# A spectral mixer and a mixture of experts on one core: where indirect DMAs, small transform pieces and logits stand in the order

## The chip, the cores and the metric

The kernel runs on one core of one Trainium2 chip, in one launch. The metric is the time of an execution on the device in microseconds (us); less is better. The time before is the median of three runs, 1420.36 us.

## The reference

```python
X = np.fft.rfft(x, axis=1)                       # x: 8 batches, 2496 tokens, 256 channels
y = np.fft.irfft(X * (filt_r + 1j * filt_i)[None], n=2496, axis=1)
x = y.reshape(8 * 2496, 256)                     # N = 19968 rows
logits = x @ w_gate                              # 8 experts
expert_idx = np.argmax(logits, axis=1)
gate_w = softmax(logits)[np.arange(N), expert_idx]
# each row goes through the one expert that it chose:
h = np.maximum(x_e @ w1[e], 0.0)                 # 256 -> 1024
y_e = h @ w2[e]                                  # 1024 -> 256
out = gate_w[:, None] * y                        # rows back in their own order
```

All of it is in float32.

## The kernel before

Each batch goes through a transform in four stages on TensorE, with the filter on VectorE and GpSimd in the middle: stage a (`bank<-fin,ta`), stage b (`bank<-fin,tb`), stage c (`bank<-zz,tc`) and stage d (`bank<-fin,td`). Batches 2 to 7 use half-size forms of these stages, whose matmuls fill a part of the array each, so that several run side by side: 64x64 tiles for a and d ("quarter" in the code), 64x32 and 32x64 tiles for b and c ("eighth"). A batch has 22 tiles of tokens, in six chunks of up to four. After stage d, each chunk of these batches is transposed on VectorE (`turn_y`, `yt`), multiplied by the gate's weights in 128x32 tiles (`block_logits`, `bank<-yt,wb`, "row" in the code), copied out of PSUM (`ls`) and turned back by a small matmul (`block_back`, `bank<-sel,ls`). Every two chunks, `route` finds the experts, gates and places of 8 tiles of tokens, and each tile's rows are scattered to a table in DRAM sorted by expert (`rows<-yo,row`): a small copy puts the gate into the row (`yo<-gts`, on ScalarE or GpSimd), and GpSimd issues an indirect DMA. When a batch is scattered, `tile_map` makes the list of expert tiles that are now full, in a chain of operations on 1x8 to 1x40 elements on VectorE (`av_i`, `av`, `end`, `add`, `past`, `erow`, `rrow`).

Expert tiles of up to 512 rows follow: SyncE loads rows (`xg`) and weights (`w1t`, `w2t`), VectorE turns the rows (`xT`), GpSimd makes sums of weights (`wsum`), TensorE makes the products (`bank<-xT,w1t`, `bank<-sums,wsum`, `bank<-xT,wsum`, `bank<-w2t,hT`), and result rows (`ys`) go to the output by an indirect DMA from GpSimd (`out_dram<-ys,ng`). These products are TensorE's filler: while batch k is transformed, tiles of batches before it are multiplied. Behind the last batch's scatters only expert tiles are left.

All engines take their instructions in the order in which this program writes them. A planner (class `Order`) sets the order while it is written: it keeps an estimated time for each engine and each tile, and the main loop takes the step that is due and ready by these estimates. `DUE` is a table of some 60 numbers: due times of the steps and thresholds. Four parts of the planner matter here. `count` estimates what an instruction takes. `flush` issues stores, and result DMAs once their rows are ready by the estimate (or four are waiting). `side` advances `route`, and halts it at a scatter while GpSimd's estimated time is over `DUE["side"]` ahead of TensorE's. The main loop picks the next step; if the last one was of a small shape, a step of the same shape goes first (`same`). The page gives line 484 for every instruction (484 is the helper through which the planner issues), so tiles' names are used instead.

Of the kernel before, what the change touches and what calls it, by code (L numbers as in the profile page):

```python
# [20 lines left out]
P = 128  # L21
# [194 lines left out]
def most_pieces(groups):  # L216
# [11 lines left out]
    "rush": -48.714,  # L228
    "alike": 0.017917,
    "mix": 25.552,  # L230
    "x_engine": 0.28811,
    "h_engine": 0.86204,
    "w2_engine": 0.11423,
    "f_engine": 0.085965,
    "gate_engine": 1.019,
    "flush": 0.57109,
    "send": 0.29959,
    "side": 2.3746,
    "idle": 2.8515,
    "share_most": 5.3092,  # L240
    "share_least": 1.471,
    "share_kept": 315.71,
    "tile": 35.828,
    "planes_by": 0.76561,
    "planes": -0.87134,
    "signs_by": 0.33611,
    "signs": -0.1406,
    "late_b": 0.31336,
    "late_s": 0.55053,
    "late_c": 0.040383,  # L250
    "filter": 0.021597,
    "filter_by": 0.0482,
    "third": 0.29655,
    "filter_ahead": 0.73168,
    "early_b": -0.23633,
    "early_by": 1.3308,
    "early_c": 0.020642,
    "first_0": -0.32219,
    "first": -0.06639,
    "first_by": 0.85692,  # L260
    "fold": 0.1218,
    "fold_ahead": 0.16979,
    "fourth_0_by": 0.87411,
    "fourth_0": 0.23401,
    "fourth_1": 0.42245,
    "fourth": 0.32009,
    "fourth_by": 0.78703,
    "turn": -0.083147,
    "logits": 0.013028,
    "back": 0.010872,  # L270
    "later_0": 0.22158,
    "later": 0.066514,
    "lists_0": 1.5128,
    "lists": 1.1508,
    "x_ahead": 0.71159,
    "stored": 0.7191,
    "w1_sums": 0.67379,
    "h_sums": 2.3401,
    "w2_sums": 1.2229,
    "w2_pace": 2.1142,  # L280
    "begin": 1.4709,
    "same": 0.30193,
# [3 lines left out]
class Order:  # L286
# [9 lines left out]
    PORT = 0.13  # L296

    def __init__(self, nc):
# [6 lines left out]
        self.kind = ""  # L305
        self.done, self.used, self.slots, self.ahead = {}, {}, {}, {}
# [77 lines left out]
    def count(self, engine, op, args, named):  # L384
# [25 lines left out]
        if op.endswith("dma_start"):  # L410
# [6 lines left out]
            self.t[engine] = start + self.ISSUE[engine]  # L417
            took = self.transfer(out, named["in_"]) * (1.1544 if engine == "gpsimd" else 1.0)
# [7 lines left out]
        elif engine == "tensor":  # L426
# [105 lines left out]
def kernel(  # L532
# [584 lines left out]
    def block_logits(b, c):  # L1117

        n = CH[c][1]
        yt = yts.pop((b, c))  # L1120
        lt = bank()[:, :n * CT]
        for r in range(2):
            for q in range(4):
                j = 4 * r + q
                mm(lt[q * CT:(q + 1) * CT], lhsT=wb[:, j, :], rhs=yt[:, :, j * CT:(j + 1) * CT], start=(r == 0), stop=(r == 1))
        ls = outs["s", b, c] = sb.tile([P, 4 * CT], F32, tag="ls", name="ls", bufs=1)[:, :n * CT]
        evac(ls, lt, n * CT)

    def block_back(b, c):

        n = CH[c][1] * CT
        p = bank()[:n, :CT]
        mm(p, lhsT=outs.pop(("s", b, c)), rhs=sel, start=True, stop=True)
        evac(lgs[b][:n, 4 * c:4 * c + 4].rearrange("p i e -> p (i e)"), p, CT)
# [28 lines left out]
    def route(b, c0, c1):  # L1163
# [670 lines left out]
    def slot(k):  # L1834
# [48 lines left out]
        if k + 1 < B:  # L1883
            for c in range(nch):
                at = (DUE["first_0"] if k == 0 else DUE["first"]) + DUE["first_by"] * c / nch
                late_x = k + 1 >= BA
                if late_x:
                    steps.append((max(at - DUE["fold"], 0.001), lambda c=c: fold_x(k + 1, c), ("x", k + 1, c), 0.0, "x", lambda c=c: t["vector"] < t["tensor"] + DUE["fold_ahead"] and [ins["x", k + 1, c]]))
                steps.append((max(at, 0.002), lambda c=c: stage_a(k + 1, c), None if late_x else ("x", k + 1, c), (0.29 if late_x else 0.43) * CH[c][1], "a",
                              lambda c=c: (not late_x or (k + 1, c) in folded) and [tables["ta"], ins["x", k + 1, c], sb.free("st") - 0.9]))  # L1890
                if late_x:
                    KINDS[steps[-1][1]] = "quarter"
        if k > 0:
            for c in range(nch + 3):
# [10 lines left out]
                if by_blocks(k - 1):  # L1905
                    if 1 <= c <= nch:
                        steps.append((at + DUE["turn"], lambda c=c: turn_y(k - 1, c - 1), None, 0.0, "d", lambda c=c: len(yts) < 2 and ("odd", k - 1, c - 1) not in outs and [outs["o", k - 1, c - 1]]))
                        steps.append((at + DUE["logits"], lambda c=c: block_logits(k - 1, c - 1), None, 0.5, "l", lambda c=c: [yts[k - 1, c - 1]]))
                        KINDS[steps[-1][1]] = "row"
                        steps.append((at + DUE["logits"] + DUE["back"], lambda c=c: block_back(k - 1, c - 1), None, 0.15, "l", lambda c=c: [outs["s", k - 1, c - 1]]))  # L1910
                        if c % 2 == 0:
                            steps.append((at + DUE["logits"] + DUE["back"] + 0.0005, lambda c=c: sides.append(route(k - 1, c - 2, c)), None, 0.0, "l"))
# [63 lines left out]

    def side():

        while sides and not (held[0] == "pool" and t["gpsimd"] > t["tensor"] + DUE["side"]):
# [211 lines left out]
    with tc.manual_schedule(engines=None):  # L2191
# [38 lines left out]
        while fs or any(heads):  # L2230
# [79 lines left out]
```

## Time and profile before

| | |
|---|---|
| median of three runs | 1420.36 us (1420.33 to 1420.42) |
| the profiled execution | 1419.16 us |
| its span, first instruction to last | 1417.3 us |
| TensorE busy with matmuls | 1355.6 us (96%) |
| VectorE, GpSimd, ScalarE busy | 905.5, 801.3, 579.8 us |
| indirect DMAs on GpSimd, rows scattered and results | 176 and 153 |

The page lists the busy time of each engine and the costliest groups of instructions. A matmul's end is modelled and overlaps the next one's start, so the time that a group takes of TensorE is read as the distance from its start to the start of what follows. The chain that ended last says nothing here: it holds only the last output DMA. What can be read are TensorE's own waits, stretches where its groups take longer than the same groups elsewhere, and its granted clock.

### The profile page before, as it was taken

Reading aid. Unit: us, or ns where it says so; the run is one execution under the profiler, and the core shown is the slowest. Engines: PE = TensorE matmul, PEld = TensorE weight load, DVE = VectorE, ACT = ScalarE, POOL = GpSimd, SP = SyncE. Lnnn points to the kernel's source line nnn. Section 1 sums busy time; section 2 is a strip of 40 time slices with the busy share of each in tenths; the row PEclk is TensorE's granted clock in tenths of the full one; section 3 lists DMA queues with packets and bytes.
Section 4 is the critical chain, followed back from the end, with each engine's and each line's share of the span. In section 5 each row is a group of like instructions: output and inputs, shape, how many; then the busy total and the mean of one; then the engine's idle time right before and its main releaser. Section 6 shows DMA issues by size and latency. Waiting matters only on the chain. (4 is left out here: it accounts for less than half of the span.)

```text
span 1417.3 us, 28606 instructions
## 1 busy us (share of the span) xinstructions
PE 1355.6 (96%) x9706; PEld 1052.9 (74%) x9706; DVE 905.5 (64%) x1717; ACT 579.8 (41%) x1451; POOL 801.3 (57%) x1084
## 2 busy tenths in 40 slices
PE   8998879999999989999999999998999999999997
PEld 6664546767766767767876787787888888999997
DVE  4756778657877866877767656354554455545674
ACT  3556325434444434435434344343333333344433
POOL 3436664756565368547756663665555554444465
PEclk9999999999999999999999999999999999999999
DMA  8967769569866965685574654566777646654342
GB/s 322 301 184 258 249 219 264 180 184 277 240 209 191 273 194 185 184 259 165 184 225 148 179 172 140 150 180 240 232 224 223 218 147 194 189 190 117 105 151 69
DMA packets 209717, 283.96 MB, mean 200 GB/s; under 512 B 116692, under 2 KB 154431, under 8 KB 209566
## 3 DMA queue, kind: packets, MB, share of 16 engines
q1 hardware_dynamic: 192510, 237.41, 55.4%
q0 software_dynamic: 17056, 44.67, 8.7%
q8 instruction: 79, 1.29, 0.4%
q14 instruction: 72, 0.59, 0.1%
HBM read 202.67 MB, written 79.60 MB: 199 GB/s over the span
## 5 line engine op out<-in xcount | busy, mean ns | idle before, releaser
L484 PE MATMUL bank<-w2t,hT 128*128 128x256 f32 (+1 forms) x2592 | 471.2, 336 | 1.0 <-DVE w2t L484 0.5
L484 PEld LDWEIGHTS bank<-w2t,hT 128*128 128x128 f32 x2592 | 407.7, 191 | 54.7 <-issue 8.0
L484 DVE TENSOR_TENSOR hT<-bank,hT 128x512 f32<-128x512 f32 (+1 forms) x228 | 147.2, 659 | 217.3 <-PE bank L484 184.7
L484 POOL DMA_INDIRECT out_dram<-ys,ng x153 | 163.9, 1071 | 136.5 <-ACT ys L484 57.3
L484 POOL DMA_INDIRECT rows<-yo,row x176 | 182.9, 1039 | 83.1 <-ACT yo L484 29.9
L484 ACT ACTIVATE ys<-bank,ng 128x128 f32<-128x128 f32 (+1 forms) x206 | 80.5, 414 | 354.0 <-PE bank L484 309.1
L484 POOL TENSOR_TENSOR wsum<-w1t 128x256 f32<-128x256 f32 x152 | 126.6, 833 | 170.0 <-PE bank L484 155.0
L484 ACT COPY hT<-bank 128x512 f32<-128x512 f32 (+1 forms) x228 | 127.9, 565 | 122.0 <-PE bank L484 100.7
L484 PE MATMUL bank<-sums,wsum 128*128 128x256 f32 (+1 forms) x608 | 158.5, 383 | 11.5 <-ACT hT L484 5.6
L484 PE MATMUL bank<-xT,w1t 128*128 128x256 f32 (+1 forms) x672 | 157.0, 378 | 1.7 <-issue 1.4
L484 PE MATMUL bank<-xT,wsum 128*128 128x256 f32 (+1 forms) x608 | 154.0, 376 | 1.4 <-DVE hT L484 1.3
L484 PEld LDWEIGHTS bank<-xT,w1t 128*128 128x128 f32 x672 | 121.5, 193 | 27.6 <-issue 7.4
L484 ACT ACTIVATE hT<-hT 128x512 f32<-128x512 f32 (+2 forms) x152 | 123.6, 813 | 42.6 <-DVE hT L484 41.0
L484 PEld LDWEIGHTS bank<-sums,wsum 128*128 128x128 f32 x608 | 103.9, 191 | 46.4 <-issue 24.2
L484 PEld LDWEIGHTS bank<-xT,wsum 128*128 128x128 f32 x608 | 109.1, 192 | 24.2 <-issue 8.2
L484 ACT ACTIVATE hT<-bank 128x512 f32<-128x512 f32 (+2 forms) x141 | 64.3, 468 | 43.8 <-PE bank L484 40.8
L484 PE MATMUL bank<-sums,w1t 128*128 128x256 f32 (+1 forms) x304 | 75.8, 372 | 0.6 <-ACT hT L484 0.6
L484 POOL TENSOR_TENSOR wsum<-wsum,w1t 128x256 f32<-128x256 f32 x76 | 65.0, 855 | 6.0
L484 POOL TENSOR_TENSOR wsum<-w1t,wsum 128x256 f32<-128x256 f32 x76 | 63.2, 832 | 0.0
L484 PEld LDWEIGHTS bank<-sums,w1t 128*128 128x128 f32 x304 | 54.7, 192 | 10.3 <-ACT hT L484 1.4
L484 DVE SCALAR_TENSOR_TENSOR ys<-bank,ng,ys 128x128 f32<-128x128 f32 x84 | 26.2, 346 | 54.8 <-PE bank L484 35.6
L484 DVE TENSOR_TENSOR sums<-xT,sums 128x256 f32<-128x256 f32 (+1 forms) x76 | 59.6, 785 | 1.9
(191 smaller groups left out, 1914.2 us busy)
## 6 DMA issues: line engine op xcount, KB each, us to landing
w1t<-in_moe_w_dram SPq DMA_DIRECT2D x80, 512.0 KB
w2t<-in_moe_w_dram SPq DMA_DIRECT2D x80, 512.0 KB
fin<-in_x_dram SPq DMA_DIRECT2D x39, 512.0 KB
fin<-zd SPq DMA_DIRECT2D x35, 512.0 KB
xg<-rows SPq DMA_DIRECT2D x136, 128.0 KB
ud<-uo SPq DMA_DIRECT2D x30, 512.0 KB
zd<-zo SPq DMA_DIRECT2D x31, 480.0 KB
fin<-ud SPq DMA_DIRECT2D x24, 512.0 KB
```

What stands on the lines that cost most here:

```text
L484: return real(*args, **named)
```

## The change

1. The planner notes indirect DMAs on GpSimd: one that starts less than 1.6 us after the one before continues a run (`trains`). Small-shape matmuls near a run are estimated longer, by a table (`TRAIN`).
2. In the main loop, steps of the "eighth" and "row" shapes are put last in the choice while a run of two or more stands near TensorE's time, and the preference for the same shape is off then.
3. A scatter of `route`, and a result DMA while transform steps are left, also waits, in the planner's time, until a gap after the indirect DMA before has passed (`paced`): 1.3223 us for batches 0 and 1, 2.4431 us for the others. No semaphore or delay is added on the chip: only the place in the order changes. `hold` exists too, but with its threshold of 99 it never holds.
4. `block_logits` and `block_back` take two chunks at a time: 18 visits in place of 36 each, with the same matmuls; one copy out of PSUM in place of two for the logits.
5. Stage a of a folded pair of chunks waits for both folds. The cost of a change of shape depends on the shape (`SWITCH`), and all numbers of `DUE` are new.

The matmuls and the bytes moved are the same; 25 of the gate copies go from ScalarE to GpSimd, and a few additions change places between VectorE and GpSimd.

```diff
 DUE = {
+    "train": 1.5001,
+    "hold": 99,
+    "pace": 2.4431,
+    "pace_0": 1.3223,
...
-    "logits": 0.013028,
+    "logits": 0.046351,
...
+    TRAIN = {"": (1.0, 1.0, 1.0, 1.12, 1.12, 2.55), "row": (1.36, 1.16, 1.66, 1.66, 1.66, 1.66),
+             "quarter": (1.0, 1.0, 1.0, 1.0, 1.0, 1.0), "eighth": (1.0, 2.6, 3.25, 3.25, 3.25, 3.25)}
+    gap = 0.0
+    SWITCH = {"": 0.09, "row": 0.15, "quarter": 0.3, "eighth": 0.41}
...
+            if engine == "gpsimd":
+                at, n = self.trains[-1]
+                self.trains = self.trains[-9:] + [(start, n + 1 if start - at < 1.6 else 1)]
+                self.paced = start + self.gap
...
-                took += 0.12
+                took += self.SWITCH[self.kind]
...
+            at, n = next((r for r in reversed(self.trains) if r[0] <= start), (-9.0, 0))
+            if n and start - at < 1.35:
+                took *= self.TRAIN[kind][min(n, 6) - 1]
...
-        while sends and (nc.ready(sends[0][0]) <= t["tensor"] + DUE["send"] or len(sends) > 3):
+        while sends and (max(nc.ready(sends[0][0]), nc.paced if fs else 0.0) <= t["tensor"] + DUE["send"] and not hold() or len(sends) > 3):
             send()
...
     def block_logits(b, c):
...
+        for i in range(c, c + 2):
+            n = CH[i][1]
+            yt = yts.pop((b, i))
+            for r in range(2):
+                for q in range(4):
+                    j = 4 * r + q
+                    mm(lt[q * CT:(q + 1) * CT, at:at + n * CT], lhsT=wb[:, j, :], rhs=yt[:, :, j * CT:(j + 1) * CT], start=(r == 0), stop=(r == 1))
+            at += n * CT
...
+        nc.gap = DUE["pace_0"] if b < 2 else DUE["pace"]
+        yield "pool"
...
-        while sides and not (held[0] == "pool" and t["gpsimd"] > t["tensor"] + DUE["side"]):
+        while sides and not (held[0] == "pool" and (max(t["gpsimd"], nc.paced) > t["tensor"] + DUE["side"] or hold())):
...
+            trains = sum(t["tensor"] - 1.35 < at < t["tensor"] + 0.5 and n > DUE["train"] for at, n in nc.trains)
+            if trains:
+                choice.sort(key=lambda c: not isinstance(c[0], int) and KINDS.get(c[0][1]) in ("eighth", "row"))
...
-            if same:
+            if same and not (trains and nc.kind in ("eighth", "row")):
```

Three places show how the order moves. In the rows, `xN` counts equal instructions that follow each other.

TensorE, in the part of the program where batch 2's first stage-d pieces stand (`fin,td`), before:

```order
L484 MATMUL bank<-xT,w1t 128x256 x10
L484 MATMUL bank<-w2t,hT 128x256 x16
L484 MATMUL bank<-fin,td 64x512 x4
L484 MATMUL bank<-fin,ta 64x512 x8
L484 MATMUL bank<-fin,td 64x512 x4
L484 MATMUL bank<-yt,wb 32x128 x8
L484 MATMUL bank<-xT,w1t 128x256 x4
L484 MATMUL bank<-fin,ta 64x512 x4
L484 MATMUL bank<-fin,td 64x512 x4
```

And the same part now:

```order
L500 MATMUL bank<-fin,ta 64x512 x8
L500 MATMUL bank<-w2t,hT 128x256 x8
L500 MATMUL bank<-fin,td 64x512 x4
L500 MATMUL bank<-xT,w1t 128x256 x4
L500 MATMUL bank<-fin,td 64x512 x4
L500 MATMUL bank<-sums,wsum 128x256 x2
L500 MATMUL bank<-xT,wsum 128x256 x2
L500 MATMUL bank<-sums,wsum 128x256 x2
L500 MATMUL bank<-sums,w1t 128x256 x2
L500 MATMUL bank<-xT,w1t 128x256 x4
L500 MATMUL bank<-fin,td 64x512 x4
```

The first logits (`yt,wb`), which stood right behind the second stage-d piece, are no longer in this stretch: they come with nine rows between them and the second stage-d piece, as 16 matmuls of two chunks together; expert products stand between the stage-d pieces.

GpSimd, in the same part of the program, from the last scatter of batch 1 on (`zp`, `zz`: the filter's products; `xT`, `wsum`: sums for expert tiles), before:

```order
L484 DMA rows<-yo,row 163840x264
L484 TENSOR_TENSOR zp<-zz,hl 128x1024
L484 TENSOR_TENSOR zz<-zz,hl 128x1024
L484 TENSOR_TENSOR zp<-zp,zz 128x512 x2
L484 DMA out_dram<-ys,ng 19968x256
L484 MEMSET lg 64x32
L484 DMA out_dram<-ys,ng 19968x256
L484 TENSOR_TENSOR zp<-zz,hl 128x1024
L484 TENSOR_TENSOR zz<-zz,hl 128x1024
L484 TENSOR_TENSOR xT<-xT 128x256
```

And now:

```order
L500 DMA rows<-yo,row 163840x264
L500 MEMSET tau_77 1x1
L500 DMA out_dram<-ys,ng 19968x256
L500 MEMSET tau_77 1x1
L500 DMA out_dram<-ys,ng 19968x256
L500 TENSOR_TENSOR xT<-xT 128x256
L500 TENSOR_TENSOR wsum<-w1t 128x256
L500 TENSOR_TENSOR wsum<-wsum,w1t 128x256
```

Between the last scatter and the sum for the next expert tile (`xT`) no filter product stands on GpSimd any more, where six operations on 512 or 1024 columns stood.

GpSimd, where the last six tiles of batch 4 are scattered, before:

```order
L484 DMA out_dram<-ys,ng 19968x256
L484 TENSOR_SCALAR yo<-lids 128x4x4
L484 TENSOR_SCALAR yo<-lids 128x2x4
L484 DMA rows<-yo,row 163840x264
L484 MEMSET tau_77 1x1
L484 DMA rows<-yo,row 163840x264
L484 MEMSET tau_77 1x1
L484 DMA rows<-yo,row 163840x264
```

And now:

```order
L500 DMA out_dram<-ys,ng 19968x256
L500 TENSOR_SCALAR yo<-lids 128x4x4
L500 TENSOR_SCALAR yo<-lids 128x2x4
L500 COPY yo<-gts 128x4
L500 DMA rows<-yo,row 163840x264
L500 TENSOR_TENSOR wsum<-w1t 128x256
L500 TENSOR_TENSOR wsum<-wsum,w1t 128x256
L500 TENSOR_TENSOR wsum<-w1t 128x256
L500 TENSOR_TENSOR wsum<-w1t,wsum 128x256
L500 DMA out_dram<-ys,ng 19968x256
L500 COPY yo<-gts 128x4
L500 DMA rows<-yo,row 163840x264
```

The six scatters followed each other with only a one-element memset between them. Now a set of weight sums and a result DMA stand behind the first, and gate copies on GpSimd before the first and the second; the four others still follow with a memset or a gate copy between.

## Rows read from the trace of the kernel before

**Rows 1.** The page's first part: each engine's busy time, its share of the span and its instructions.

```profile
PE 1355.6 (96%) x9706; PEld 1052.9 (74%) x9706; DVE 905.5 (64%) x1717; ACT 579.8 (41%) x1451; POOL 801.3 (57%) x1084
```

**Rows 2.** The table of windows, stretches of 100 us: each engine's busy time with its instructions in brackets, then the granted TensorE clock (1.00 is 2.4 GHz, 0.50 is 1.2 GHz), DMA share and GB/s.

```profile
100.00:200.00 100.00, 89.41 (x585) 52.27 (x583) 70.50 (x169) 46.18 (x146) 65.00 (x105) 0.95 0.73 238
...
1200.00:1300.00 100.00, 100.00 (x684) 92.61 (x683) 53.66 (x85) 38.34 (x89) 44.98 (x59) 1.00 0.57 174
```

**Rows 3.** The view of waits, TensorE alone: the instruction that waited and whom it waited for, then us in total, number of waits, longest wait. "issue" is a wait for nothing that the profile shows.

```profile
PE bank L484 <- issue: 13.2, 11, 4.0
PE bank L484 <- DVE yt L484: 8.5, 2, 8.1
PE bank L484 <- ACT hT L484: 6.5, 7, 4.0
```

**Rows 4.** Groups of TensorE instructions by shape, 100 to 450 us: tile shape in the array, operand, count of records (two records make one matmul), then busy us, mean ns of one, and idle time before them.

```profile
L484 PE MATMUL bank<-fin,tb 64*32 64x512 f32 x224 | 21.9, 605 | 1.4 <-issue 1.1
...
L484 PE MATMUL bank<-zz,tc 32*64 32x512 f32 x192 | 14.3, 654 | 0.2 <-issue 0.2
...
L484 PE MATMUL bank<-fin,tb 64*32 64x256 f32 x96 | 5.3, 388 | 0.9 <-issue 0.8
...
L484 PE MATMUL bank<-zz,tc 32*64 32x256 f32 x96 | 3.7, 387 | 0.0
```

**Rows 5.** The same view of the same four shapes, 560 to 900 us.

```profile
L484 PE MATMUL bank<-fin,tb 64*32 64x512 f32 x128 | 8.6, 599 | 0.0
L484 PE MATMUL bank<-zz,tc 32*64 32x512 f32 x128 | 7.9, 600 | 0.0
...
L484 PE MATMUL bank<-zz,tc 32*64 32x256 f32 x96 | 3.4, 387 | 0.0
L484 PE MATMUL bank<-fin,tb 64*32 64x256 f32 x80 | 3.3, 388 | 0.0
```

**Rows 6.** The timeline, 411 to 418 us, GpSimd's indirect DMAs and one second-stage piece of the transform on TensorE: start, us, engine, what, count, in brackets the idle time before.

```profile
412.91 0.96 POOL L484 DMA_INDIRECT rows<-yo,row  x1 [0.25 <-issue]
...
413.44 1.79 PE L484 MATMUL bank<-fin,tb 64*32 64x256 f32 x15
...
414.18 0.96 POOL L484 DMA_INDIRECT rows<-yo,row  x1 [0.23 <-issue]
...
416.01 0.37 PE L484 MATMUL bank<-fin,tb 64*32 64x256 f32 x1 [0.78 <-issue]
```

**Rows 7.** The timeline, 966 to 985 us: the last of nine indirect DMAs in a row on GpSimd, and TensorE and ScalarE beside them.

```profile
975.01 1.03 PE L484 MATMUL bank<-xT,wsum 128*128 128x256 f32 x4
...
977.53 0.99 POOL L484 DMA_INDIRECT out_dram<-ys,ng  x1 [0.22 <-issue]
...
979.36 0.59 ACT L484 COPY hT<-bank 128x512 f32<-128x512 f32 x1 [5.43 <-remote]
...
980.00 1.54 PE L484 MATMUL bank<-sums,wsum 128*128 128x256 f32 x4 [3.96 <-issue]
```

**Rows 8.** The timeline, 184 to 214 us: VectorE's small operations that make a batch's list of tiles (av, add), GpSimd's filter products, the loads of the rows that the list names, and TensorE up to the first product on them.

```profile
189.76 3.01 DVE L484 CAST av<-av_i 1x8 f32<-1x8 int32 x1
...
192.89 2.30 DVE L484 SCALAR_TENSOR_TENSOR add<-av,done 1x8 f32<-1x8 f32 x1
...
195.25 2.50 POOL L484 TENSOR_TENSOR zp<-zp,zz 128x512 f32<-128x512 f32 x2
...
199.71 1.96 SPq L484 DMA_DIRECT2D xg<-rows  x4
...
202.93 1.04 PE L484 MATMUL bank<-fin,td 64*64 64x512 f32 x8
...
210.70 1.23 DVE L484 STREAM_TRANSPOSE yt<-yo 128x1024 f32<-128x1024 f32 x1
...
212.08 1.08 PE L484 MATMUL bank<-yt,wb 128*32 128x128 f32 x16 [8.11 <-DVE yt L484]
```

**Rows 9.** The timeline of TensorE alone, 741 to 749 us: a start less the start before it is what a group takes of TensorE's time.

```profile
742.21 0.64 PE L484 MATMUL bank<-yt,wb 128*32 128x128 f32 x16
742.78 1.97 PE L484 MATMUL bank<-zz,tc 32*64 32x512 f32 x32
744.68 1.09 PE L484 MATMUL bank<-fin,tb 64*32 64x512 f32 x16
745.70 1.13 PE L484 MATMUL bank<-xT,wsum 128*128 128x256 f32 x4
746.67 0.30 PE L484 MATMUL bank<-sel,ls 128*128 128x32 f32 x2
746.91 1.09 PE L484 MATMUL bank<-fin,tb 64*32 64x512 f32 x16
```

**Rows 10.** The same view, 655 to 660 us.

```profile
657.05 1.95 PE L484 MATMUL bank<-fin,tb 64*32 64x512 f32 x32
658.93 0.30 PE L484 MATMUL bank<-sel,ls 128*64 128x32 f32 x2
```

**Rows 11.** The table of windows, columns as above, two stretches at the lower clock.

```profile
209.00:216.00 7.00, 3.92 (x23) 3.04 (x24) 6.08 (x9) 0.85 (x2) 6.31 (x8) 0.51 1.00 356
...
980.60:984.00 3.40, 3.40 (x10) 2.65 (x9) 1.38 (x2) 0.65 (x2) 2.98 (x6) 0.50 1.04 415
```

**Rows 12.** Groups of GpSimd's instructions, 100 to 900 us: columns as in the groups above.

```profile
L484 POOL DMA_INDIRECT rows<-yo,row x161 | 167.9, 1043 | 76.2 <-ACT yo L484 27.4 <-issue 26.4 <-POOL yo L484 6.0
```

More of the change, by code (lines that the diff above doesn't have):

```diff
@@ L227 @@
 DUE = {
[L228 to L268, printed above, removed]
@@ L269 @@
-    "logits": 0.013028,
[L270 to L282, printed above, removed]
+    "train": 1.5001,
+    "hold": 99,
+    "pace": 2.4431,
+    "pace_0": 1.3223,
+    "rush": -65.48,
+    "alike": 0.0054238,
+    "mix": 25.896,
+    "x_engine": 0.31921,
@@ new lines @@
+    "h_engine": 0.85416,
+    "w2_engine": -0.0033164,
+    "f_engine": 0.46732,
+    "gate_engine": 0.74439,
+    "flush": 0.74894,
+    "send": 0.2157,
+    "side": 2.9017,
+    "idle": 2.3547,
+    "share_most": 5.534,
+    "share_least": 2.0258,
+    "share_kept": 180.9,
+    "tile": 36.383,
+    "planes_by": 0.71361,
+    "planes": -0.99615,
+    "signs_by": 0.20372,
+    "signs": -0.19037,
+    "late_b": 0.32279,
+    "late_s": 0.5423,
+    "late_c": 0.015411,
+    "filter": -0.027997,
+    "filter_by": 0.049301,
@@ new lines @@
+    "third": 0.23776,
+    "filter_ahead": 0.58338,
+    "early_b": -0.25329,
+    "early_by": 1.359,
+    "early_c": 0.050366,
+    "first_0": -0.48058,
+    "first": -0.060795,
+    "first_by": 0.86105,
+    "fold": 0.12991,
+    "fold_ahead": 0.27381,
+    "fourth_0_by": 1.0457,
+    "fourth_0": 0.24053,
+    "fourth_1": 0.55483,
+    "fourth": 0.38026,
+    "fourth_by": 0.74859,
+    "turn": -0.063865,
+    "logits": 0.046351,
+    "back": 0.037074,
+    "later_0": 0.30529,
+    "later": 0.037954,
@@ L283 @@
+    "lists_0": 1.4973,
+    "lists": 1.2957,
+    "x_ahead": 1.267,
+    "stored": 0.67267,
+    "w1_sums": 1.757,
+    "h_sums": 3.0113,
+    "w2_sums": 1.5326,
+    "w2_pace": 2.8013,
+    "begin": 1.2652,
+    "same": 0.477,
 }
@@ L305, in __init__ @@
         self.kind = ""
+        self.trains, self.paced = [(-9.0, 0)], 0.0
         self.done, self.used, self.slots, self.ahead = {}, {}, {}, {}
@@ L1117, in block_logits @@
     def block_logits(b, c):
[L1119 to L1127, printed above, removed]
-    def block_back(b, c):
[L1131 to L1134, printed above, removed]
+        lt = bank()
+        at = 0
+        for i in range(c, c + 2):
[6 more added lines that the diff above has]
+            at += n * CT
+        ls = outs["s", b, c] = sb.tile([P, 8 * CT], F32, tag="ls", name="ls", bufs=1)[:, :at]
+        evac(ls, lt[:, :at], at)
+    def block_back(b, c):
+        p = bank()
+        ls = outs.pop(("s", b, c))
+        ns = [CH[i][1] * CT for i in (c, c + 1)]
+        for i, n in enumerate(ns):
+            mm(p[:n, i * CT:(i + 1) * CT], lhsT=ls[:, i * P:i * P + n], rhs=sel, start=True, stop=True)
+        to = lgs[b][:, 4 * c:4 * c + 8].rearrange("p i e -> p (i e)")
+        if ns[0] == ns[1]:
+            evac(to, p[:, :2 * CT], 2 * CT)
+        else:
+            for i, n in enumerate(ns):
+                evac(to[:n, i * CT:(i + 1) * CT], p[:n, i * CT:(i + 1) * CT], CT)
     def logits(b, g):
@@ L1889, in slot @@
                 steps.append((max(at, 0.002), lambda c=c: stage_a(k + 1, c), None if late_x else ("x", k + 1, c), (0.29 if late_x else 0.43) * CH[c][1], "a",
-                              lambda c=c: (not late_x or (k + 1, c) in folded) and [tables["ta"], ins["x", k + 1, c], sb.free("st") - 0.9]))
+                              lambda c=c: (not late_x or {(k + 1, c), (k + 1, c | 1)} <= folded) and [tables["ta"], ins["x", k + 1, c], sb.free("st") - 0.9]))
                 if late_x:
@@ L1975, with hold @@
     held = [None]
+    def hold():
+        at, n = nc.trains[-1]
+        return nc.kind in ("eighth", "row") and n > DUE["hold"] and max(t["gpsimd"], t["tensor"]) - at < 1.6
     def side():
-        while sides and not (held[0] == "pool" and t["gpsimd"] > t["tensor"] + DUE["side"]):
+        while sides and not (held[0] == "pool" and (max(t["gpsimd"], nc.paced) > t["tensor"] + DUE["side"] or hold())):
             try:
```

6 lines of the change are left out of this document (3 added, 3 removed).

## The prediction

> **What bounds the kernel now.** TensorE does. It is busy 1355.6 of 1417.3 us and no other engine passes 905.5 [rows 1]. The matmuls are the same before and after, so the change can only take away, or add, time in which TensorE waits or goes slowly. I read the windows first: from 1200 to 1300 us, where expert tiles alone run, TensorE is busy for 100.00 of 100 us at a granted clock of 1.00, but from 100 to 200 us for 89.41 at 0.95 [rows 2]. Busy time also hides stretching, so I then compared one shape of matmul in two parts of the run [rows 4, 5], looked at what GpSimd did beside the slow ones [rows 6, 7], and went to TensorE's longest waits [rows 3, 8]. The part behind the last batch's scatters, from about 985 us on, has nearly the same order of TensorE's work in both kernels, so I count nothing there: what is won or lost before it moves the end by as much.
>
> **Small pieces beside indirect DMAs.** The records of the 64x32 pieces of 512 columns take 21.9 us for 224 before 450 us, 0.098 us each, and 8.6 us for 128 after 560 us, 0.067 each [rows 4, 5]: 224 x 0.031 = 6.9 us. In the same way the 32x64 pieces of 512 columns give 192 x (0.0745 - 0.0617) = 2.5, the 64x32 pieces of 256 columns 96 x (0.0552 - 0.0413) = 1.3, the last shape 96 x (0.0385 - 0.0354) = 0.3; the idle time before these groups adds 1.4 + 0.2 + 0.9 = 2.5. Sum: 13.5 us. What stood beside them shows at 413 us: GpSimd issues scatters at 412.91 and 414.18, each 1.27 us after the one before, and a piece begun at 413.44 gives its last matmul only at 416.01, after 0.78 us of idle time for nothing that the profile shows [rows 6]. That the run of DMAs is the cause is an inference. The change steers both sides: these pieces are put last in the choice while a run stands near, and DMAs are spaced in the planner's time. But no delay exists on the chip. Where nothing else stands between two DMAs, GpSimd can issue the second at 1.27 us, whatever the planner thought; the order of batch 4's last scatters still has four nearly in a row. Some of the stretch is also clock: from 100 to 200 us it is 0.95 [rows 2]. Bounds: 0 and -13.5. I take **-8**, more than half, since the choice of TensorE's step is steered too, not the DMAs alone.
>
> **Large matmuls in long runs.** After nine DMAs in a row TensorE stands idle for 3.96 us up to 980.00, ScalarE for 5.43 up to 979.36, both without a reason in the profile [rows 7], and then the clock is 0.50 for 3.4 us [rows 11], which costs 1.7. All such waits of TensorE's sum to 13.2 us [rows 3], 2.5 of which are counted above. These runs come when padding rows and results are sent behind the last scatters, which the pace of the scatters doesn't touch, and the results only while transform steps are left. Bounds: 0 and -6; I take **-2**.
>
> What the rows of 980 us show is that two engines stop at once beside a run of DMAs. The Trainium skill, "Runtime: NRT & Kernel Launch", section "Instruction fetch mechanics", speaks against a loss of this kind: each engine's instructions are refilled ahead by DMA, and the cost of a refill is called mostly hidden. The trace disagrees at this one place, if refills are what stopped here, which no run here shows. By the page these two terms would be 0.
>
> **Logits in pairs.** 18 visits of each of two shapes fall away: 6 batches x 6 chunks, halved. What a visit costs is read from a shape that stands with 16 and with 32 records: 744.68 to 745.70 is 1.02 us [rows 9], 657.05 to 658.93 is 1.88 [rows 10]; so the second 16 cost 0.86 and a visit 0.16 by itself. For the turning back (`sel,ls`), two records take 746.67 to 746.91, 0.24 us [rows 9]; two more in the same visit I estimate at 0.11, a little under half of that, so 0.13 is saved. 18 x (0.16 + 0.13) = 5.2. Copies out of PSUM fall away too, on ScalarE, which is busy 579.8 us [rows 1]: nothing. A pair waits for its second chunk, but stands later in the order with expert products ahead of it. Bounds -2.5 and -5.2; I take **-5**.
>
> **The wait at 204 us.** TensorE's longest named wait is 8.1 us, for the first logits' transposed chunk [rows 3]. The rows tell how it arises. VectorE makes the tile list behind batch 1's last scatter; a cast of 8 elements takes 3.01 us and an addition 2.30, beside GpSimd's filter products [rows 8]. So the rows of the next expert tile are requested at 199.71, and VectorE turns the logits' chunk behind that tile's work, at 210.70; TensorE, which has nothing but logits next, stands until 212.08 [rows 8], and the clock is 0.51 from 209 to 216 us, where 3.92 us of work cost half of that more [rows 11]: about 10 us in all. In the new order no filter product stands on GpSimd between the last scatter and that tile's sum, and on TensorE expert products stand between the stage-d pieces and logits come much later. What is late next there is the first expert product, if the tile's rows come as late as before. Bounds 0 and -10; I take **-8**.
>
> **The rest of the order.** All due times are new, so every wait that was small by luck is dealt again. An own wait of the old order such as the 6.5 us for `hT` [rows 3] can go as well as come, and new ones are not in this trace. Bounds 0 and +20 (two waits like the one of 10 us); I take **+5**, less than one. 25 more gate copies on GpSimd lie beside its idle time: its scatters alone waited 76.2 us [rows 12]. Folds in pairs and the terms of `SWITCH` issue no instruction.
>
> **Sum.** -8 - 2 - 5 - 8 + 5 = -18 us. The profiled execution took 1419.2 us, 1.9 of them outside the span; the median is 1.2 above it. 1419.2 - 18 + 1.2 = 1402.4, so **1402 us**. With all lower bounds -13.5 - 6 - 5.2 - 10 = -35 (1386), with all upper ones -2.5 + 20 = +18 (1438).
>
> **Rivals.**
> 1. *The distance is not kept on the chip.* GpSimd runs behind its order and issues paced DMAs 1.27 us apart again. For it: GpSimd issues that fast whenever it has DMAs in its order [rows 6], and nothing holds it. Against it: scatters also wait for gate copies on ScalarE, 27.4 us before 161 scatters [rows 12], and these copies follow TensorE's pace. Then the first two terms are 0 and -5 - 8 + 5 = -8: 1412 us.
> 2. *Runs are not what slows the pieces*, and stretches come from something that the change leaves alone, such as the load on all DMA queues before 450 us (DMA share 0.73 from 100 to 200 us [rows 2], 0.57 in the late window). For it: the late part has scatters too and is calm [rows 5]. Against it: the coincidence of rows 6. Also 1412 us. By the Trainium skill's section cited above ("Runtime: NRT & Kernel Launch", "Instruction fetch mechanics") refills would not be what runs slow there; no run here shows it.
> 3. *Slower: expert tiles starve.* Paced scatters end later in a batch, its list is made later, rows come later, and TensorE stands at that batch's first products as it did at 204 us. Price: 10 us a batch [rows 8, 11]. Without the 204-us term the gains are -15; so it decides from two of the six late batches on, and with three it is +15: 1435 us. For it: batch 4's last scatters now stand behind weight sums. Against it: other tiles' products are in stock at that point, and rows are loaded only when the planner holds them ready.
> 4. *No change*: one or two such waits eat the gain, 1417 to 1423 us.
>
> **How the numbers follow.** Forecast 0.58, rival 1 0.17, rival 2 0.05, rival 3 0.11, no change 0.09. The range runs from 1388, as two terms reach their lower bounds, to 1420, which takes in rivals 1 and 2 and half of no change; about 0.07 lies below and 0.13 above. A measurement of this kernel tells about 0.2%, 2.8 us, from no change. Faster by more than that: 0.57 of the forecast, 0.15 and 0.04 of the first two rivals, 0.76. Within: 0.12. Slower: 0.12, nearly all rival 3.
>
> **What would show it.** In the profile after: the 64x32 pieces of 512 columns before 450 us near 0.067 us a record, and not 0.098; no wait of 8 us for `yt`; `yt,wb` in groups of 32 records; the clock at 1.00 from 200 to 220 us. If 64x32 pieces are as slow as before, rival 1 or 2 holds, and starts of scatters 1.27 us apart beside them tell which. A wait of TensorE for `xT` or `hT` at the first products of several batches would be rival 3, and the forecast would be wrong.

## The result, and the profile after

The changed kernel took 1397.76 us (median of 5 runs, 1396.76 to 1399.22) against 1420.36 for the kernel before on the same chip (5 runs, 1415.15 to 1423.07): a ratio of 0.9845, 95% interval 0.9823 to 0.9867, or 22.6 us less. The prediction was 1402 us, faster. The profiled execution took 1396.76 us.

The first part of the page of the changed kernel, which answers to [rows 1], and its slices of TensorE's clock:

```profile
span 1395.0 us, 28518 instructions
...
PE 1346.1 (96%) x9706; PEld 1052.6 (75%) x9706; DVE 908.1 (65%) x1722; ACT 575.2 (41%) x1390; POOL 816.8 (59%) x1096
...
PEclk9998999999999999999999999999999999999999
```

TensorE executes the same 9706 records. Its busy time fell from 1355.6 to 1346.1 us (-9.5) and the rest of the span from 61.7 to 48.9 (-12.8): stretching and waiting both went down.

TensorE's waits in the changed kernel, the view of [rows 3]:

```profile
PE bank L500 <- DVE hT L500: 8.1, 6, 2.5
PE bank L500 <- issue: 6.4, 12, 1.0
PE bank L500 <- POOL w2t L500: 3.9, 1, 3.9
PE bank L500 <- POOL zz L500: 3.8, 2, 3.0
```

The wait of 8.1 us for `yt` is gone, and the waits for nothing that the profile shows are halved (13.2 to 6.4, the longest 4.0 to 1.0). Those for `hT` from VectorE grew (3.2 us in all before), those for `zz` from GpSimd a little (2.8 before), and one for `w2t`, also on GpSimd, is new.

The four small shapes of the transform, 100 to 450 us, the view of [rows 4]:

```profile
L500 PE MATMUL bank<-fin,tb 64*32 64x512 f32 x224 | 17.6, 623 | 1.1 <-issue 0.8
L500 PE MATMUL bank<-zz,tc 32*64 32x512 f32 x192 | 15.1, 668 | 3.8 <-POOL zz L500 3.8
L500 PE MATMUL bank<-fin,tb 64*32 64x256 f32 x96 | 6.2, 385 | 0.6
...
L500 PE MATMUL bank<-zz,tc 32*64 32x256 f32 x96 | 4.7, 387 | 0.8 <-issue 0.7
```

The first shape is faster (0.098 to 0.079 us a record; 0.067 in the calm stretch), the others are not, and the idle time before them grew from 2.5 to 6.3 us. Where TensorE's work stood at about 204 us before, the windows and the timeline of TensorE now read:

```profile
100.00:200.00 100.00, 87.02 (x571) 47.59 (x573) 61.78 (x171) 45.13 (x140) 61.84 (x102) 0.95 0.72 229
200.00:220.00 20.00, 18.23 (x108) 11.99 (x104) 19.26 (x24) 8.61 (x15) 16.87 (x15) 1.00 1.01 297
```

```profile
214.75 1.09 PE L500 MATMUL bank<-fin,td 64*64 64x512 f32 x8
216.91 1.10 PE L500 MATMUL bank<-xT,wsum 128*128 128x256 f32 x4 [1.07 <-DVE hT L500]
...
219.67 1.08 PE L500 MATMUL bank<-yt,wb 128*32 128x128 f32 x32
```

The clock is 1.00 from 200 to 220 us (0.51 from 209 to 216 before, [rows 11]), expert products (`xT,wsum`) stand between the stage-d piece and the logits, and the logits run as 32 records. The stretch from 100 to 200 us is no better than in [rows 2]: 87.02 us busy against 89.41, at the same clock.

To see where the time came from, every unbroken group of records on TensorE is given the time to the start of the next group, and the time that its records take in calm stretches (the lower quartile of the same shape) is taken off. What is left, the loss, is 22.3 us smaller in the changed kernel, as the span is. Laid against equal amounts of TensorE's work done, it is 2.0 us larger in the first 150 us of work, 9.6 smaller in the next 50 (the wait at 204 us), 0.4 smaller from 200 to 300, 10.1 smaller from 300 to 500, and 4.2 smaller in all the rest.

### The profile page after: what moved, and what is told of

It reads as the page before. It is cut to its first block, busy times and chain, and to the rows that moved or that the text cites. A ratio compares the mean times of both kernels' runs of the same rounds, so it can differ in the third digit from the quotient of the medians.

```text
span 1395.0 us, 28518 instructions
## 1 busy us (share of the span) xinstructions
PE 1346.1 (96%) x9706; PEld 1052.6 (75%) x9706; DVE 908.1 (65%) x1722; ACT 575.2 (41%) x1390; POOL 816.8 (59%) x1096
## 5 line engine op out<-in xcount | busy, mean ns | idle before, releaser
L500 POOL DMA_INDIRECT rows<-yo,row x176 | 186.2, 1058 | 73.0 <-issue 30.3
L500 DVE TENSOR_TENSOR sums<-xT,sums 128x256 f32<-128x256 f32 (+1 forms) x76 | 63.6, 837 | 1.9
L500 DVE COPY uo<-bank 128x512 f32<-128x512 f32 (+1 forms) x35 | 19.7, 596 | 67.6 <-PE bank L500 64.9
```

What stands on the lines that cost most here:

```text
L500: return real(*args, **named)
```

## Experiments

The experiments ran on five chips, and the first thing they show is that these chips differ. The kernel before took 1389.39 us on one (20 runs) and 1390.51 on another (17), and 1420.92 (17), 1428.98 (17) and 1432.89 (9) on three more. Below, "a 1390 chip" and "a 1420 chip" stand for the two kinds. Each chip was measured in one stretch of time, so a lasting condition of a chip can't be told from the chip itself; the granted clock explains little of the kinds (0.989 in the profile of x_pairs, 0.985 in that of x_pairs_b below, which on 1400 us is an estimated 6 of the 40 us between them). Ratios are always to the kernel before on the same chip.

| kernel | on a 1390 chip | on a 1420 chip |
|---|---|---|
| changed kernel | not measured | 0.9845 [0.9823, 0.9867]; x_after_b 0.9809 [0.9788, 0.9829] |
| before, pairs alone | x_pairs 0.9987 [0.9975, 0.9998] | x_pairs_b 0.9998 [0.9981, 1.0015] |
| changed, no distance | x_nopace 1.0030 [1.0012, 1.0048]; x_nopace_b 1.0023 [0.9999, 1.0047] | not measured |
| changed, no holding back | x_notrain 1.0122 [1.0101, 1.0143] | not measured |
| changed, neither | x_neither 1.0057 [1.0036, 1.0077] | x_neither_b 1.0185 [1.0157, 1.0213] |
| before, filter moved | not measured | x_filter 0.9992 [0.9979, 1.0006] |
| before, one number nudged | not measured | x_side_before 0.9937 [0.9923, 0.9950] |
| before / changed, DMAs spread by memsets | not measured | x_far_before 1.1364, x_far_after 1.1292 |

Undoing one part makes the planner deal the whole order anew, so such a kernel differs from its base in more than the part. Only x_filter and the two x_far kernels keep the order of their base on every engine.

**x_pairs and x_pairs_b: the pairs alone.** The kernel before with the change's `block_logits`, `block_back` and their steps:

```diff
+        for i in range(c, c + 2):
+            yt = yts.pop((b, i))
...
-    steps.append((at + DUE["logits"], lambda c=c: block_logits(k - 1, c - 1), ...
+    if c % 2 == 0:
+        steps.append((at + DUE["logits"], lambda c=c: block_logits(k - 1, c - 2), ...
```

> The kernel before with the logits of two blocks made together and nothing else; its table of numbers and planner are the old ones, but the planner deals the order anew, since steps fell away. The six filter operations on GpSimd still stand beside the list chain in front of the 204 us wait. My theory (the gain of 22.6 us is the wait at 204 us, some 8 to 12, the pairs, some 3 to 5, and an order that by chance or by the new numbers waits less): 1412 to 1418 us, with the 8 us wait for yt still in the trace and yt,wb in runs of 32 records. Rival (the distance between the indirect DMAs and the holding back of small pieces bring the gain): 1418 to 1422. Rival (any newly dealt order is worth as much as the change): below 1405.

> The kernel before with the logits in pairs alone, as in x_pairs. On a chip where the kernel before takes 1389 us it was level with it (ratio 0.9987), and theory A expects 0.997 to 1.0 there again. On a chip where the kernel before takes 1420: theory A (distance and holding back are needed where the pieces are stretched): 1410 to 1420 us; theory B (pairs and a newly dealt order): 1395 to 1408.

1387.94 us on a 1390 chip, 1428.02 on a 1420 chip: level with the kernel before on both, to within 0.3%. No 8 us wait for `yt` is left in either, against my expectation, but x_pairs waits 7.9 us for `xT`, 6.7 for `zp` and 6.6 for `fin`, and x_pairs_b 13.8 for `hT`. On the 1420 chip the time lies above both ranges that I had given. The same program with the same order takes 40 us more on one chip than on the other, and its two profiles say where. Groups of TensorE's instructions by shape in x_pairs:

```profile
L484 PE MATMUL bank<-zz,tc 32*64 32x512 f32 x384 | 24.6, 600 | 0.0
L484 PE MATMUL bank<-fin,tb 64*32 64x512 f32 x384 | 24.1, 597 | 0.0
...
L484 PE MATMUL bank<-w2s,hT 128*32 128x256 f32 x320 | 18.3, 380 | 0.0
```

and in x_pairs_b:

```profile
L484 PE MATMUL bank<-fin,tb 64*32 64x512 f32 x384 | 32.7, 598 | 0.3
...
L484 PE MATMUL bank<-zz,tc 32*64 32x512 f32 x384 | 24.6, 600 | 0.0
L484 PE MATMUL bank<-w2s,hT 128*32 128x256 f32 x320 | 21.8, 382 | 0.3
```

`fin,tb` takes 0.063 us a record on the 1390 chip, about as in the calm stretch of [rows 5] (0.067), and 0.085 on the other. `zz,tc` is the same on both, although most of it stands beside indirect DMAs too (5.7 of its 24 us beside the third or a later one of a run), so not every piece is stretched there. Matched group by group, all `fin,tb` groups make up 14.8 of the 40 us, `w2s,hT` 3.9, and full-size products (`xT,w1t` 6.8, `w2t,hT` 4.1, `xT,wsum` 3.4) much of the rest. Sorted by what GpSimd did beside them on the 1390 chip, groups that overlap the third or a later DMA of a run (264 us of TensorE's time) took 21.6 us longer on the other chip, those beside a first or second one (426 us) 10.0, all others (694 us) 7.6. The DMA engines as a whole were as busy on either, a share of 0.74 and 0.70 from 100 to 450 us.

**x_nopace and x_nopace_b: no distance.** In the changed kernel:

```diff
-    "pace": 2.4431,
-    "pace_0": 1.3223,
+    "pace": 0.0,
+    "pace_0": 0.0,
```

> The changed kernel with no distance between the indirect DMAs in its planner (both paces zero), all other numbers kept; the order is dealt anew. My theory (the planner's distance hardly reaches the chip: 116 of 239 indirect DMAs start within 1.6 us of the one before, 121 of 230 in the kernel before): 1395 to 1403 us, the share of close starts at most 10 points higher, the eighth-tile pieces as slow as now. Rival (the distance brings the gain): 1405 to 1412, and the 64x32 pieces between 100 and 450 us slower by 4 us or more.

> The changed kernel without the distance between indirect DMAs, holding back kept, as in x_nopace (1395.6 us on the chip where the kernel before takes 1389). There 202 of its 277 indirect DMAs between 100 and 1010 us stood in runs of three or more on the chip and 149 in runs of six or more; the changed kernel has 143 and 62, the kernel before 179 and 49. Theory A1 (on a chip where the kernel before takes 1420 us or more, runs cost, and the distance is what shortens them): ratio above 1.0, 1425 to 1465 us, with halts of several engines in the long runs. Theory A2 (it is enough that small pieces are kept away from runs; the distance adds little): 0.980 to 0.992, 1395 to 1420 us. On a chip where the kernel before takes 1389 us: 1.001 to 1.006 by both.

1395.64 and 1393.08 us, both on 1390 chips, 0.3 and 0.2% above the kernel before (the second interval takes in 1). What the distance does on the chip can be counted: of the indirect DMAs between 100 and 1010 us, 199 of 277 stand in runs of three or more (starts less than 1.6 us apart), in the changed kernel 141 of 278, in the kernel before 177 of 278 (the expectation above counts runs that begin before 100 us whole). Part of my expectation, that the distance hardly reaches the chip, rested on counting all close pairs and was wrong. What the distance alone is worth on a 1420 chip stays open.

**x_notrain: no holding back.** In the changed kernel:

```diff
-    "train": 1.5001,
+    "train": 99,
...
-    TRAIN = {"": (1.0, 1.0, 1.0, 1.12, 1.12, 2.55), "row": ...
+    TRAIN = dict.fromkeys(("", "row", "quarter", "eighth"), (1.0,) * 6)
```

> The changed kernel whose planner does not hold small pieces back during runs of indirect DMAs and does not reckon them as slower there; the distance, the pairs and the numbers are kept; the order is dealt anew. My theory: 1395 to 1406 us, since the small pieces became hardly faster in the changed kernel (45.2 to 43.6 us busy in the four eighth shapes between 100 and 450 us, with 3.8 us more idle time before them), and what it loses stands as a wait at one place, not in these pieces. Rival (holding back is what pays): 1408 to 1415, with these four shapes back at 45 us or above.

1406.61 us on a 1390 chip, 1.2% above the kernel before there: more than I expected as a ratio; the microseconds of both expectations were meant for a 1420 chip. Its longest wait is one that the other kernels don't have:

```profile
PE bank L499 <- DMA xr<-rows: 11.1, 1, 11.1
```

That is TensorE at the start of the part behind the last batch, which makes up most of the 17 us. I take it for an accident of the new order; no run shows that. So the time says little on the holding back.

**x_neither and x_neither_b: pairs and new numbers alone.** Both edits together.

> The changed kernel with neither the distance nor the holding back: pairs and the new table of numbers alone. My theory: 1396 to 1408 us, most of the gain kept, and no wait of 8 us for yt, since fewer filter operations stand on GpSimd beside the list chain. Rival (the two mechanisms for the indirect DMAs bring the gain): 1412 to 1418, the gain of the pairs alone.

> The changed kernel without distance and without holding back: pairs and the new table of numbers alone, as in x_neither (which took 1.0057 times the kernel before on the chip where that takes 1389 us). Theory A (where small pieces are stretched beside indirect DMAs, the gain comes from the planner's keeping them apart): on a chip where the kernel before takes 1420 us or more, a ratio of 0.992 to 1.005, half of the gain or less. Theory B (the gain is a newly dealt order that waits less at a few places, the wait at 204 us above all, and the two mechanisms carry little): 0.980 to 0.990. On a chip where the kernel before takes 1389 us both expect 1.003 to 1.008, as before.

1399.64 us on a 1390 chip, 0.6% above the kernel before; 1459.54 on a 1420 chip, 1.9% above it. My first expectation, most of the gain kept, was wrong. So the order that the new numbers give without the two mechanisms is worse than the old one on both kinds of chip, and far worse where runs of DMAs hurt: 3.8% above the changed kernel (1.0185 / 0.9809, on two 1420 chips), some 54 us. That lies outside both ranges, on the side of theory A and beyond the size that I gave it. The two are a pair of profiles of one program, so the same place can be laid side by side. x_neither, the timeline of GpSimd and TensorE:

```profile
173.76 1.95 PE L499 MATMUL bank<-fin,tb 64*32 64x512 f32 x32
175.64 5.45 PE L499 MATMUL bank<-xT,w1t 128*128 128x256 f32 x24
...
173.94 0.99 POOL L499 DMA_INDIRECT rows<-yo,row  x1 [0.22 <-issue]
...
175.23 1.02 POOL L499 DMA_INDIRECT out_dram<-ys,ng  x1 [0.22 <-issue]
```

x_neither_b:

```profile
185.69 4.44 PE L499 MATMUL bank<-fin,tb 64*32 64x512 f32 x23
190.28 2.55 PE L499 MATMUL bank<-fin,tb 64*32 64x512 f32 x9 [0.16 <-issue]
192.76 1.56 PE L499 MATMUL bank<-xT,w1t 128*128 128x256 f32 x6
...
185.61 1.02 POOL L499 DMA_INDIRECT out_dram<-ys,ng  x1 [0.22 <-issue]
...
186.93 1.00 POOL L499 DMA_INDIRECT rows<-yo,row  x1 [0.26 <-issue]
```

The 32 records take 1.88 us (173.76 to 175.64) on one chip and 7.07 (185.69 to 192.76) on the other, both in a run of indirect DMAs some 1.3 us apart. Over the whole program, matched and sorted as above, groups beside the third or a later DMA of a run make up 49.2 of the 53.9 us by which the two profiles differ, in 267 us of TensorE's time. Full-size work is hit too, in longer runs. x_neither_b at 910 us, the timeline:

```profile
913.20 0.96 POOL L499 DMA_INDIRECT rows<-yo,row  x1 [0.22 <-issue]
...
915.59 0.37 ACT L499 COPY yo<-bank 128x256 f32<-128x256 f32 x1 [5.63 <-remote]
...
916.60 1.10 PE L499 MATMUL bank<-sums,wsum 128*128 128x256 f32 x4 [2.86 <-ACT yo L499]
```

and x_neither at the same place of the program:

```profile
870.44 0.38 ACT L499 COPY yo<-bank 128x256 f32<-128x256 f32 x1 [1.12 <-PE bank L499]
...
872.92 1.03 PE L499 MATMUL bank<-sums,wsum 128*128 128x256 f32 x4
```

ScalarE stands for 5.63 us, until after GpSimd's run has ended, where on the other chip it stands for 1.12 and waits for TensorE. Within the run GpSimd keeps its pace on both; its next scatter, at 916.82, waits 2.58 us for ScalarE's copy.

**x_filter: the six filter operations beside the list chain on VectorE instead of GpSimd**, in the kernel before:

```diff
+        if b == 3 and scattered[0] == 2 * NG and not on_vector:
+            return unseen(o, x, y, op)      # nc.vector, not counted by the planner
         (nc.vector if on_vector else nc.gpsimd).tensor_tensor(o, x, y, op=op)
```

> The kernel before with the same order on every engine, but the six filter operations that stood on GpSimd between 190 and 207 us are issued to VectorE at the same place in the program. My theory (VectorE's short operations of the list chain, 3.01 and 2.30 us instead of 0.16 and 0.18, are held while GpSimd's tensor operations run, and through them xg, td and yt come late): the chain from av_i to done takes about 3 us instead of 9.8 and the wait of TensorE at 204 us falls from 8.1 to 0 to 4 us, though VectorE gets some 8 us of filter work in return; time 1412 to 1417 us. Rival (the chain waits for something else, an engine's queue or a transfer): the long CAST and add stay, and the time is 1420 to 1428.

1420.51 us: no change. The timeline of x_filter, VectorE and TensorE:

```profile
189.37 0.16 DVE L484 CAST av<-av_i 1x8 f32<-1x8 int32 x1
...
189.66 0.14 DVE L484 SCALAR_TENSOR_TENSOR add<-av,done 1x8 f32<-1x8 f32 x1
...
206.52 1.30 DVE L484 STREAM_TRANSPOSE xT<-xg 128x512 f32<-128x512 f32 x2
...
209.37 1.23 DVE L484 STREAM_TRANSPOSE yt<-yo 128x1024 f32<-128x1024 f32 x1
...
210.75 1.08 PE L484 MATMUL bank<-yt,wb 128*32 128x128 f32 x16 [9.10 <-DVE yt L484]
```

Half of my theory holds: the cast takes 0.16 us instead of 3.01 and the addition 0.14 instead of 2.30, so VectorE's small operations were held by GpSimd's filter products, and the list is made 7 us faster. But TensorE waits longer than before, 9.10 us. `yt` still stands behind `xT` in VectorE's order, and VectorE, with 6.2 us of filter more (191.76 to 195.47 and 202.80 to 205.31), works without a gap from 200.87 to the end of `yt`. So the run put about as much work on VectorE ahead of `yt` as it took delay away, and whether the slow list had a part in the wait stays open. What it shows is that a fast list alone, with `yt` behind `xT` in the order, doesn't remove it.

The changed kernel has both at once: its list is fast, and its order another. Its VectorE:

```profile
187.20 0.16 DVE L500 CAST av<-av_i 1x8 f32<-1x8 int32 x1
...
201.83 1.30 DVE L500 STREAM_TRANSPOSE xT<-xg 128x512 f32<-128x512 f32 x2
...
209.93 1.23 DVE L500 STREAM_TRANSPOSE yt<-yo 128x1024 f32<-128x1024 f32 x1
```

and in the kernel before:

```profile
207.85 1.30 DVE L484 STREAM_TRANSPOSE xT<-xg 128x512 f32<-128x512 f32 x2
```

`yt` comes no earlier than before to speak of (209.93 against 210.70), but the expert tile's rows are turned 6 us earlier, and the products that TensorE makes on them (`xT,w1t` at 205.59, `sums,wsum` at 209.29) stand ahead of the logits.

**x_far_before and x_far_after: distance made on the chip**, the order of each base kept:

```diff
         if nc.sent:
             nc.gpsimd.memset(tau0[:, 31:], 0.0)
+            for _ in range(12 if fs else 0):
+                nc.nc.gpsimd.memset(tau0[:, 31:], 0.0)
```

> The kernel before with the same order on every engine and twelve more one-element memsets on GpSimd between consecutive indirect DMAs while transform steps are left, which the planner does not see: the distance is made on the chip. Theory of the change (runs of indirect DMAs slow the small pieces, distance frees them): starts within 1.6 us of one another almost gone, the four eighth shapes between 100 and 450 us 5 to 10 us less busy, time 1405 to 1416. My theory after the result (distance is worth little as such): the pieces beside runs get faster, but the scatters end later and lists, tiles and their first products wait: 1416 to 1428. Third (runs do not slow the pieces): the shapes keep 45 us, time 1420 to 1430.

> The changed kernel with the same twelve memsets between consecutive indirect DMAs, order kept. Theory of the change: 1385 to 1395 us, the four eighth shapes between 100 and 450 us 5 to 10 us below their 43.6. My theory: the pieces gain some us and waits for the lists take as much or more: 1396 to 1408. Third (runs do not slow the pieces): shapes unchanged, 1398 to 1410.

1614.05 and 1603.97 us, 14 and 13% slower: no expectation came near. Twelve memsets put the DMAs 3.54 us apart (133.56 to 137.10 in x_far_before), and GpSimd's other work then comes late. TensorE's largest waits in x_far_before:

```profile
PE bank L484 <- POOL wsum L484: 44.4, 7, 11.8
PE bank L484 <- DVE yt L484: 40.7, 2, 40.4
PE bank L484 <- POOL zz L484: 29.1, 2, 15.1
```

No run of three is left, and `fin,tb` of 512 columns, 100 to 450 us, falls from 0.098 to 0.076 us a record (12.2 us for 160), although the mean clock of the whole run is 0.928 instead of 0.989. The DMA engines are less busy there as well (a share of 0.56 from 100 to 450 us instead of 0.74), so this run alone doesn't tell the runs from the load; the twin profiles do. Delay made on GpSimd is no cure here.

**x_side_before: one number nudged**, an order dealt anew by chance, in the kernel before:

```diff
-    "side": 2.3746,
+    "side": 2.34,
```

> The kernel before with one number of its table nudged by 1.5 per cent (side 2.3746 to 2.34), which deals the order anew: what an order as such is worth. If the table had been chosen among many by time, a nudge costs: 1420 to 1432 us. If orders are worth as much as the change itself, the time lies 10 us or more from 1420.

1411.92 us, 0.6% faster than the kernel before. 9 us of 22.6 can come from an order as such, so no single term below can be told from luck when it is smaller than about that. Its waits for `yt` are shorter too (5.0 us in all, 3.4 at most).

**x_after_b: the changed kernel again**, no edit.

> The changed kernel, unaltered. On the chip of the first four experiments the kernel before took 1389 us instead of 1420, and its small-tile products stood at their length without traffic beside runs of indirect DMAs (no w2s,hT visit over by 0.75 us there, four of them elsewhere, in the part whose order is the same). Theory A (what the change gains is mostly that it meets this stretching less, so it is worth most where the stretching is): on a chip where the kernel before takes 1420 us, 1395 to 1400; on one where it takes 1389, 1383 to 1395, a ratio of 0.995 to 1.004. Theory B (the gain is waits and pairs, whatever the chip): ratio 0.98 to 0.99 on either, 1362 to 1375 us where the kernel before takes 1389.

1401.24 us on a chip where the kernel before takes 1428.98. It repeats the first result; the changed kernel on a 1390 chip, which would tell the theories apart, is not measured.

## Why the prediction was right, term by term

**Total.** -18 us was forecast, -22.6 measured: right in sign and nearly in size. The terms are another matter, and that they add up is in part luck: x_pairs_b has the logits in pairs and no 8 us wait for `yt`, two terms that make -13 together, and is level with the kernel before on its chip.

**Small pieces beside indirect DMAs, -8.** That such pieces are stretched beside runs is shown by the twin profiles above: the same pieces in the same order, on one chip and not on the other. The step that failed is where the gain was to come. In the four shapes that I priced, before 450 us, busy and idle time went from 47.7 to 49.9 us: no gain; 3.8 us of it is a wait for `zz`. The sign that I had named, 0.067 us a record, came half-way, at 0.079. Over all groups of tiles at most 64 columns wide that overlap the third or later DMA of a run, from 100 to 1010 us, the loss went from 17.7 us on 20.2 us of work to 9.6 on 10.3: -8.1. That this is the number forecast is luck; drawn otherwise (the four shapes alone, all small tiles, a narrower or wider "beside") it comes out between -1 and -9. It took both mechanisms to halve the work beside runs: 20.4 us without holding back (x_notrain), 26.0 without distance (x_nopace), 16.6 with neither. For scale, x_neither_b loses 24.1 us on 17.2 there, and x_neither, the same program on a 1390 chip, 2.1 on 16.6.

**Large matmuls in long runs, -2.** Not seen in its place: full-size groups at the sixth or later DMA of a run lost 5.4 us before and 5.5 after. At the place of [rows 7] the halt without a reason is gone, and a wait as long with a reason has come:

```profile
973.12 1.26 POOL L500 TENSOR_TENSOR w2t<-w2t 128x512 f32<-128x512 f32 x1
...
974.44 3.32 PE L500 MATMUL bank<-w2t,hT 128*128 128x128 f32 x16 [3.94 <-POOL w2t L500]
...
977.80 0.63 ACT L500 ACTIVATE ys<-bank,ng 128x128 f32<-128x128 f32 x2 [5.99 <-PE bank L500]
```

TensorE waits 3.94 us for `w2t`, which GpSimd makes behind the weight sums that follow its run of DMAs, and ScalarE then waits for TensorE. That the pace doesn't touch these runs was predicted. Beside them I cited the Trainium skill, "Runtime: NRT & Kernel Launch", section "Instruction fetch mechanics", by which refills of instructions are mostly hidden. Between 184 and 194 us of x_neither_b, where 32 records took 7.07 us, the transfers by queue are:

```profile
DMA packets 674, 1.99 MB, mean 199 GB/s; under 512 B 160, under 2 KB 199, under 8 KB 674
...
q1 hardware_dynamic: 352, 1.31, 42.1%
q0 software_dynamic: 322, 0.67, 18.4%
```

No packet of the two queues that the page of the profile lists as instruction (q8 and q14) is among them, and TensorE went on without one, so refills are not what stopped it there; nor is there one from 909 to 916 us, where ScalarE stood. At the halt of [rows 7] there is one; from 974 to 980 us of the kernel before the same view has

```profile
q14 instruction: 1, 0.01, 0.3%
```

It stands at 979.60, after ScalarE's return at 979.36 and before TensorE's at 980.00, so there a refill can't be ruled out for TensorE. What stopped the engines is not settled.

**Logits in pairs, -5.** At their own place they brought two thirds of what was priced: `yt,wb` and `sel,ls` of all widths took 29.7 us of TensorE before and 26.5 after (-3.2, within -2.5 to -5.2). By themselves they brought the kernel nothing that can be measured (0.9987 and 0.9998). The step that failed is counting a local gain as a gain of the end when the same edit deals the order anew.

**The wait at 204 us, -8.** Gone, with its clock; the loss shrank by 9.6 us there, near the forecast and within its bounds. Of my account of its cause the runs leave the first link open: x_filter made the list fast and kept the wait, but with other work on VectorE in its place. In the changed kernel all links changed at once: the list is fast, the tile's rows are turned 6 us earlier, and expert products stand on TensorE ahead of the logits.

**The rest, +5.** What the other four leave of the 22.3 us is about -1.5, if none of them overlap. New waits came (`hT` +4.9, `w2t` 3.9, `zz` +1.0) and old ones went (`hT` from ScalarE 6.5 to 2.6, "issue" 13.2 to 6.4). The 10.1 us won from 300 to 500 us of work were placed there by no term of mine. The largest losses of the kernel before in that part, which the changed one lacks, are a wait of 4.0 us for `hT` up to 523 us, one of 2.8 for `zz` up to 556 us, and the piece of [rows 6] at 413 us with the product behind it, 3.7 over their calm time.

**The rivals.** 1, distance not kept: its sign is in the trace, slow pieces beside starts some 1.3 us apart still occur (105.86 us in the changed kernel: 4.8 us for 32 records), but runs of three or more fell from 177 to 141 DMAs. 2, runs are not the cause: it falls by the twins on a 1420 chip, where the DMA engines are no busier than on the other; on a 1390 chip it would be nearly true. 3, starving tiles: not seen. A question that none of them asked: whether the chip at hand is one where runs hurt.

**What stays open.** Whether the change gains anything on a 1390 chip: its relatives without one or both mechanisms took 1.002 to 1.012 there. How its gain on a 1420 chip divides between distance, holding back and an order that happens to wait less. What it is about a chip that makes runs stop its engines.

## What to carry to other kernels

When a change is built around a stall, find out first whether the stall belongs to the program or to the chip: run the kernel before on several chips and compare one order's profiles group by group. Where a planner deals the order, nudge one number as a control before giving a term of a few microseconds to a part. And an operation that runs slowly ahead of a wait is not its cause until taking it away takes the wait, without as much work put in the same engine's way.

## What was not expected of the hardware

- One program, one order, 1388 us on one chip and 1428 on another (x_pairs), 1400 and 1460 for a second program (x_neither). There, beside runs of indirect DMAs, TensorE's small pieces (1.88 against 7.07 us for 32 records) and ScalarE (1.12 against 5.63 us) stop on some chips, while GpSimd issues 1.3 us apart on both.
- VectorE's operations on 8 elements took 3.01 and 2.30 us beside GpSimd's tensor products and 0.16 and 0.14 without them. The Trainium skill, "GPSIMD Engine Reference", section "1. Specifications", says that GpSimd's way to SBUF is shared with VectorE and contended by some of VectorE's instructions. x_filter agrees. In the kernel before, the cast and the addition each end as a GpSimd product of 2.35 and 2.37 us beside them ends (192.77 and 192.73 us, 195.19 and 195.18), so even so small an operation can stand for as long as a product takes.
